# Two more blocks of an attention softmax moved from batched passes to head-by-head ScalarE exponentials

## The chip, the core and the metric

The kernel runs on one core of a Trainium2 chip. The metric is the device time of one execution in microseconds (us). TensorE is called PE here, its weight loads PEld, VectorE DVE, ScalarE ACT, GpSimd POOL, and SyncE, which issues most of the DMAs, SP.

## The reference

What is computed, cut to its three stages: attention over pooled keys and values, a gated feed-forward layer, and eight experts mixed by a normalised table.

```python
# 1 attention: batch 4, 8 heads, 576 queries, keys and values averaged in groups of 8 (72 left)
scores = scale * q @ k_p.T
scores = scores - max(scores, axis=-1)
attn = exp(scores); attn = attn / (sum(attn, axis=-1) + 1e-9)
x = attn @ v_p                                   # 2304 tokens x 512
# 2 gated layer: 512 -> 1536 -> 512
x = (sigmoid(x @ w_gate) * (x @ w_val)) @ w_out
# 3 eight experts of width 1024, weights P from 8 rounds of row and column normalisation
out = sum over e of P[:, e] * (relu(x @ w1[e]) @ w2[e])
```

Only the softmax of the first stage is touched by the change.

## The kernel before

Tokens are handled in six blocks of 384 (`NBLK`, `TB`), each of three tiles of 128 tokens (t = 0, 1, 2). Each tile has eight heads in two groups of four (g = 0, 1). So one block has six score groups. A score group fills 128 x 4 x 72 numbers of one PSUM bank.

All products of the gated layer are done in split precision: an operand is rounded to a high part (by ACT) and the rest is a low part (a subtraction by DVE or POOL), and `mm` does three matmuls for each pair. For a weight chunk of 128x512 the rounding is L231 (`wa_hi`) and the subtraction L236 (`wa_lo`), both in `split_chunk`. The 36 chunks of the gated layer's weights arrive as 64-bit numbers and must first be narrowed to 32 bits. That is done by `narrow_tick` in several ticks per chunk: DVE L165 to L175, an add L179 (POOL for the first 12 chunks, DVE for the others) and a scaling by ACT, L185. When a chunk has been rounded, it is also stored to DRAM (`narrow`, issued from ACT's queue) so that later blocks can read it back (`stage`).

The gated layer runs in 72 steps (j, f), block j against slice f of the hidden width. Their order begins with (0,0), (0,1), (0,2), (0,3), (1,2), (1,3), (1,0), (1,1), (2,0), (2,1); I call these steps 0 to 9. A step is: 12 matmuls for the gate ("g", L268), a sigmoid on ACT (L817), 12 for the value ("v", L268), their product on DVE (L820), its rounding on ACT (L821) and the low part on DVE (L824); then the 12 matmuls of the step before into the output (`x2_step`, L560).

The attention of block 0 runs ahead of all steps. The attention of the other blocks is a Python generator, `attention`, whose stages are slipped between the parts of the steps by `slot`, which is called three times in a step: after the sigmoid, after the value part, and after `x2_step`. In each slot first the narrowing ticks are placed, as long as an estimate of DVE's due time (`until`) is not too far ahead of PE's. Then stages are placed by credit: each slot adds (23 less the stages done) / (3 x steps left to the block's nominal first step, less the slot's number, less 3), and each stage costs one credit. `hold` can forbid stages before a given step. At the start of a step whose block isn't ready, all remaining stages of that block are placed at once. Engines work strictly in the order in which the program was written out, so this placing sets every queue's order.

The stages of a block j > 0 before the change: (for a new batch) two stages of key pooling (L320) and two of value pooling (L329); six stages `scores`, in which each stage first runs the `less_max` of the group before; then the stages of the softmax; then for each tile `divide`, two transposes (`turn_a`, L422, with a copy by ACT, L424), and `values` (L437), whose result ACT and DVE split into `xs`, which the matmuls of the block's steps read.

In `less_max`, block 0 takes the negated maximum of the group on DVE and then runs four exponentials on ACT, one for each head, straight from PSUM with the maximum as bias; each gives the row's sum as a by-product. Blocks 1 to 5 take the maximum (L369) and subtract it (L370) on DVE into the tile `e`; one exponential over the block's whole `e` (L393) is put in the list `later`, and three sums on DVE (`total`, L397), `invert` and `divide` (L407) follow.

PSUM banks for the attention while steps run come from the tag "at", which has two, used in turn; a bank comes free when its group has been read. `e` has one buffer, `den` two, and the narrowed chunk `made` four, each released by its store to DRAM.

Of the kernel before, what the change touches and what calls it, by code (L numbers as in the profile page):

```python
# [20 lines left out]
def attention_moe_moe_kernel(  # L21
# [112 lines left out]
    later = []  # L134
# [154 lines left out]
    now = [0]  # L289
    hold = [0]  # L290

    def attention(at):
        kp, vp, qs, krs, vrs = {}, {}, {}, {}, {}
        e_ts, dens, a_ts = {}, {}, {}

        def load_k(b, hp):
            krs[b, hp] = at.tile([128, SP, POOL], F32, tag="kr", name="kr", bufs=4)
            nc.sync.dma_start(
                out=krs[b, hp].rearrange("p s j -> p (s j)"), in_=k[b, :, hp * S : (hp + 1) * S]
            )  # L300

        def load_v(b, i):
            vrs[b, i] = at.tile([SP, 2 * D, POOL], F32, tag="vr", name="vr", bufs=4)
            nc.sync.dma_start(
                out=vrs[b, i].rearrange("p d j -> p (d j)"), in_=v[b, :, 2 * i * DM : 2 * (i + 1) * DM]
            )
# [8 lines left out]
        def pool_k(b, hp):  # L315

            if hp == 0:
                kp[b] = at.tile([128, HP, SP], F32, tag="kp", name="kp", bufs=2)
            until["dve"] += 750
            nc.vector.tensor_reduce(out=kp[b][:, hp], in_=krs.pop((b, hp)), axis=AX.X, op=ALU.add)  # L320
            if hp == HP - 1:
                nc.scalar.activation(out=kp[b], in_=kp[b], func=AF.Copy, scale=SCALE)

        def pool_v(b, i):

            if i == 0:
                vp[b] = at.tile([SP, DM], F32, tag="vp", name="vp", bufs=2)
            until["dve"] += 1150
            nc.vector.tensor_reduce(  # L329
                out=vp[b][:, 2 * D * i : 2 * D * (i + 1)], in_=vrs.pop((b, i)), axis=AX.X, op=ALU.add  # L330
            )
# [7 lines left out]
        def scores(j, t, g):  # L339


            if (t, g) == (0, 0):
                e_ts[j] = at.tile([128, TPB, H, SP], F32, tag="e", name="e", bufs=1)
                dens[j] = at.tile([128, TPB, H], F32, tag="den", name="den", bufs=2)
            e_t = e_ts[j][:, t, 4 * g : 4 * g + 4]
            pt = at_bank()
            sc = pt[:, 0 : 4 * SP].rearrange("p (h s) -> p h s", h=4)
            for c0, c1, b in pieces(j, t):
                for i in range(4):
                    pr = slice(64 * g, 64 * g + 64)  # L350
                    nc.tensor.matmul(  # L351
                        out=sc[c0:c1, i],
                        lhsT=qs[j, t][pr, i, c0:c1],
                        rhs=kp[b][pr, i],
                        start=True,
                        stop=True,
                    )
            if g:
                del qs[j, t]
            elif (j, t) != (0, 0):  # L360
                load_q(j + (t + 3) // TPB, (t + 3) % TPB)
            m = at.tile([128, 4], F32, tag="mx", name="mx", bufs=4)
            until["pe"] += 900
            until["dve"] += 950
            post.append(lambda: less_max(j, t, g, sc, m, e_t))

        def less_max(j, t, g, sc, m, e_t):
            if j:
                nc.vector.tensor_reduce(out=m, in_=sc, axis=AX.X, op=ALU.max)  # L369
                nc.vector.tensor_sub(out=e_t, in0=sc, in1=m.unsqueeze(2).to_broadcast([128, 4, SP]))  # L370
                return
            nc.vector.tensor_reduce(out=m, in_=sc, axis=AX.X, op=ALU.max, negate=True)
            for i in range(4):
                nc.scalar.activation(
                    out=e_t[:, i],
                    in_=sc[:, i],
                    func=AF.Exp,
                    bias=m[:, i : i + 1],
                    accum_out=dens[j][:, t, 4 * g + i : 4 * g + i + 1],
                )  # L380
# [4 lines left out]
        def flush():  # L385
            while post:
                post.pop(0)()
# [3 lines left out]
        def softmax(j):  # L391
            e_t = e_ts[j]
            nc.scalar.activation(out=e_t, in_=e_t, func=AF.Exp)  # L393

        def total(j, t):
            until["dve"] += 700
            nc.vector.tensor_reduce(out=dens[j][:, t], in_=e_ts[j][:, t], axis=AX.X, op=ALU.add)  # L397

        def invert(j, t):
            until["dve"] += 500  # L400
            den = dens[j][:, t]
            nc.vector.tensor_scalar_add(out=den, in0=den, scalar1=EPS)
            nc.vector.reciprocal(out=den, in_=den)

        def divide(j, t):
            until["dve"] += 750
            nc.vector.tensor_tensor(  # L407
                out=e_ts[j][:, t],
                in0=e_ts[j][:, t],
                in1=dens[j][:, t].unsqueeze(2).to_broadcast([128, H, SP]),  # L410
                op=ALU.mult,
            )

        def turn_a(j, t, g):

            if g == 0:
                a_ts[j, t] = at.tile([SP, H, 128], F32, tag="a", name="a", bufs=3)
            pt = at_bank()
            pa = pt[:SP].rearrange("p (h s) -> p h s", h=4)
            until["pe"] += 500  # L420
            for i in range(4):
                nc.tensor.transpose(out=pa[:, i], in_=e_ts[j][:, t, 4 * g + i], identity=ident)  # L422
            a_t = a_ts[j, t][:, 4 * g : 4 * g + 4]
            post.append(lambda: nc.scalar.copy(out=a_t, in_=pa))  # L424
# [71 lines left out]
        for j in range(1, NBLK):  # L496
            b = (j * TB + TB - 1) // S
            if (j * TB - 1) // S < b:
                for hp in range(0, HP, 2):
                    pool_k(b, hp)  # L500
                    pool_k(b, hp + 1)
                    yield None
                for i in range(4):
                    pool_v(b, i)
                    if i % 2:
                        yield None
            for t in range(TPB):
                for g in range(2):
                    scores(j, t, g)
                    yield None  # L510
                    flush()
            later.append(lambda j=j: softmax(j))
            hold[0] = now[0] + 1 + (j > 1)
            yield None
            while later:
                later.pop(0)()
            total(j, 0)
            total(j, 1)
            yield None
            total(j, 2)  # L520
            invert(j, slice(0, TPB))
            divide(j, 0)
            yield None
            divide(j, 1)
            yield None
            divide(j, 2)
            nb = ((j + 1) * TB + TB - 1) // S
            if j + 1 < NBLK and nb > b:
                for hp in range(HP):
                    load_k(nb, hp)  # L530
                for i in range(4):
                    load_v(nb, i)
            for t in range(TPB):
                for g in range(2):
                    turn_a(j, t, g)
                    yield None
                    flush()
                yield j
                values(j, t)
                if t < TPB - 1:  # L540
                    yield None
                flush()
            yield -1
# [183 lines left out]
    with tc.manual_schedule():  # L727
# [4 lines left out]
        at = at_pool.__enter__()  # L732
        pools["at"] = at
        stages = attention(at)
        mark = [None]
        n_ready = [0]
# [379 lines left out]
```

## Time and profile before

| | us |
|---|---|
| Median of 3 runs | 2191.98 |
| Lowest and highest run | 2191.56, 2198.58 |
| The profiled execution, its own time | 2192.21 |
| Span of its trace | 2190.4 |
| PE busy | 2091.4 |
| DVE busy | 1422.9 |
| ACT busy | 882.3 |
| POOL busy | 890.9 |

The profile is one execution. A busy PE is not one at its peak, so the granted clock of each stretch is read beside it: 1.0 stands for 2.4 GHz, and lower mean values of a stretch contain time at 1.2 GHz. Where an engine was idle, the trace names the engine and line that ended the wait. The 1.8 us between span and time lie outside of the trace.

### The profile page before, as it was taken

The page shows a single profiled execution, that of the slowest core. Times are in us where ns is not written, and L with a number is a line of the kernel's source. Part 1 is how long each engine was busy: PE and PEld are TensorE (multiplying, and loading weights), DVE is VectorE, ACT ScalarE, POOL GpSimd, SP SyncE. Part 2 cuts the span into 40 slices and gives each one's busy share as a digit, 9 for nine tenths or more (in the row PEclk, how much of TensorE's full clock was granted, in tenths as well). Part 3 has the DMA queues.
Part 4 walks back from the last instruction along what each step waited for, and adds up shares of the span by engine and source line. Part 5 has one row for each costly group of instructions (what it writes and reads, how often), then busy time and mean ns, then how long its engine had stood idle before and what let it go on. Part 6 is the DMA issues. An engine that isn't in the chain of part 4 may idle for free.

```text
span 2190.4 us, 28664 instructions
## 1 busy us (share of the span) xinstructions
PE 2091.4 (95%) x10973; PEld 1899.3 (87%) x10973; DVE 1422.9 (65%) x2172; ACT 882.3 (40%) x1607; POOL 890.9 (41%) x780
## 2 busy tenths in 40 slices
PE   4579998999999999999999999999999999999999
PEld 4468988988997888888888888989898989898988
DVE  6746876645434877666666666666666666666665
ACT  4234333454544344434343434343434343434342
POOL 1100000254554465454545454545454545454441
PEclk8689999999999999999999999999999999999999
DMA  7432553453572232121215121212125212121211
GB/s 228 151 112 81 164 168 106 130 172 117 191 242 75 75 116 77 58 78 58 78 58 207 58 77 58 78 58 78 58 77 180 85 58 78 58 78 58 77 58 39
DMA packets 87450, 222.09 MB, mean 101 GB/s; under 512 B 8848, under 2 KB 8848, under 8 KB 87312
## 3 DMA queue, kind: packets, MB, share of 16 engines
q1 hardware_dynamic: 82128, 210.81, 28.7%
q10 hardware_dynamic: 5184, 9.44, 1.2%
q8 instruction: 86, 1.41, 0.3%
q14 instruction: 52, 0.43, 0.1%
HBM read 189.55 MB, written 30.67 MB: 101 GB/s over the span
## 4 chain that ended last, share of the span: by engine, by line
PE 87%; DVE 7%; issue 2%; ACT 2%; DMA 1%; POOL 0%; SPq 0%; ACTq 0%; DVEq 0%; POOLq 0%
PE big L932 36%; PE at L901 18%; PE gv L901 14%; PE gv L268 11%; PE big L560 5%; DVE wa_lo L236 1%; PE at L351 1%; PE at L437 1%; DVE made L166 1%; DVE wide L175 1%; PE at L422 1%; DVE g L820 1%; DMA narrow<-made 0%; DVE den L397 0%; ACT wa_hi L231 0%
## 5 line engine op out<-in xcount | busy, mean ns | idle before, releaser
L932 PE MATMUL big<-w2hl,h 128*128 128x512 f32 x3456 | 893.7, 394 | 0.0
L932 PEld LDWEIGHTS big<-w2hl,h 128*128 128x128 f32 x3456 | 641.9, 188 | 102.6
L961 DVE SCALAR_TENSOR_TENSOR acc<-big,prob,acc 128x512 f32<-128x512 f32 x516 | 385.6, 747 | 265.2 <-PE big L932 259.1
L705 POOL TENSOR_TENSOR fa<-raw,fa 128x768 fp32r<-128x768 f32 x96 | 179.5, 1869 | 442.1 <-PE big L932 403.3
L268 PE MATMUL gv<-xs,wa_hi 128*128 128x384 f32 x1152 | 310.6, 351 | 19.5 <-ACT xs L447 8.0
L707 POOL TENSOR_TENSOR fs<-ss,fs 128x512 fp32r<-128x512 f32 x96 | 125.0, 1302 | 292.5 <-ACT fs L704 292.5
L915 ACT ACTIVATE h<-gv 128x384 fp32r<-128x384 f32 x192 | 94.3, 491 | 356.9 <-DVE gv L1043 196.2
L268 PEld LDWEIGHTS gv<-xs,wa_hi 128*128 128x128 f32 x1152 | 214.4, 196 | 26.2 <-ACT xs L447 8.8
L901 PE MATMUL at<-xf,fa 128*128 128x384 f32 x1152 | 233.4, 337 | 0.8 <-DVE c L1036 0.8
L901 PE MATMUL at<-xf,fs 128*128 128x384 f32 x1152 | 232.3, 336 | 0.4 <-ACT c L1009 0.4
L901 PE MATMUL gv<-xf,fs 128*128 128x384 f32 x1152 | 232.3, 337 | 0.0
L717 DVE TENSOR_TENSOR w2hl<-raw,w2hl 128x512 fp32r<-128x512 f32 x192 | 227.5, 1186 | 6.3 <-ACT w2hl L716 6.3
L901 PEld LDWEIGHTS at<-xf,fa 128*128 128x128 f32 x1152 | 206.4, 188 | 17.7 <-DVE c L1036 1.6
L268 PE MATMUL gv<-xs,wa_lo 128*128 128x384 f32 x576 | 200.8, 349 | 20.6 <-DVE wa_lo L236 18.6
L901 PEld LDWEIGHTS gv<-xf,fs 128*128 128x128 f32 x1152 | 206.1, 189 | 16.4 <-issue 0.2
L901 PEld LDWEIGHTS at<-xf,fs 128*128 128x128 f32 x1152 | 204.4, 188 | 9.0 <-ACT c L1009 0.7
L916 DVE SCALAR_TENSOR_TENSOR h<-gv,h 128x384 fp32r<-128x384 f32 x192 | 107.1, 558 | 107.7 <-ACT h L915 107.7
L560 PE MATMUL big<-h,wa_hi 128*128 128x384 f32 x576 | 150.8, 343 | 0.0
L594 POOL TENSOR_TENSOR fx<-x,fx 128x768 fp32r<-128x768 f32 x10 | 18.4, 1844 | 318.6 <-DVE x L577 266.8
L268 PEld LDWEIGHTS gv<-xs,wa_lo 128*128 128x128 f32 x576 | 112.9, 196 | 25.0 <-DVE wa_lo L236 22.6
L236 POOL TENSOR_TENSOR wa_lo<-stage,wa_hi 128x512 fp32r<-128x512 f32 x67 | 99.1, 1494 | 82.4 <-ACT wa_hi L231 69.0
L821 ACT ACTIVATE h<-g 128x384 fp32r<-128x384 f32 x72 | 37.8, 525 | 222.9 <-DVE g L820 222.9
(149 smaller groups left out, 2766.4 us busy)
## 6 DMA issues: line engine op xcount, KB each, us to landing
raw<-in_moe_w_dram SPq DMA_DIRECT2D x192, 512.0 KB, 4.1
stage<-narrow SPq DMA_DIRECT2D x150, 256.0 KB, 3.0
xd<-fx SPq DMA_DIRECT2D x21, 768.0 KB, 3.7
xf<-xd SPq DMA_DIRECT2D x21, 768.0 KB, 6.3
narrow<-made ACTq DMA_DIRECT2D x36, 256.0 KB, 2.6
wide<-in_moe_w_gate_dram SPq DMA_DIRECT2D x12, 512.0 KB, 3.7
wide<-in_moe_w_val_dram SPq DMA_DIRECT2D x12, 512.0 KB, 5.1
wide<-in_moe_w_out_dram SPq DMA_DIRECT2D x12, 512.0 KB, 7.4
```

What stands on the lines that cost most here:

```text
L236: eng.tensor_tensor(out=lo, in0=raw, in1=f32(hi), op=ALU.subtract)
L268: nc.tensor.matmul(out=out_, lhsT=a[s], rhs=b[m], start=(i == 0), stop=(i == n - 1))
L560: nc.tensor.matmul(out=x2p[d][:, :TB], lhsT=w[s][:, d * 128 : (d + 1) * 128], rhs=gs[j, f][m], start=(first and i == 0), stop=(last and i ...
L705: pl(out=fa[:, 1], in0=raw[:, 0:3], in1=f32(fa[:, 0]), op=ALU.subtract)
L707: pl(out=fs[:, 1, 0:2], in0=ss[:, 0:2], in1=f32(fs[:, 0, 0:2]), op=ALU.subtract)
L717: nc.vector.tensor_sub(out=t[:, 1, i], in0=raw[:, i], in1=f32(t[:, 0, i]))
L821: nc.scalar.activation(out=hi, in_=g, func=AF.Copy)
L901: nc.tensor.matmul(out=pt[:, :TB], lhsT=w[:, s, i, k], rhs=t[:, o, k], start=(start and m == 0), stop=(m == 5), skip_group_check=True,)
L915: nc.scalar.activation(out=t[:, 0], in_=src, func=AF.Relu)
L916: nc.vector.scalar_tensor_tensor(out=t[:, 1], in0=src, scalar=0.0, in1=f32(t[:, 0]), op0=ALU.max, op1=ALU.subtract)
L932: nc.tensor.matmul(out=py, lhsT=h[:, s, cs], rhs=w2hl[n][:, o, fh], start=(m == 0), stop=(m == 5))
L961: nc.vector.scalar_tensor_tensor(out=acc[t], in0=py, scalar=pr, in1=acc[t], op0=ALU.mult, op1=ALU.add)
```

## The change

Blocks 1 and 2 take the way of block 0: `less_max` now compares j with a constant `WHOLE` = 3. For these two blocks the subtraction on DVE is gone; four exponentials on ACT read the score bank, with the maximum as bias, and give the sums. The block-wide exponential, the three sums, their place in `later` and the `hold` are gone for them, and so is one of the two stages that held them; the other is left as an empty `yield`. Blocks 3 to 5 are as before.

```diff
     def attention(at):
+        WHOLE = 3
 ...
         def less_max(j, t, g, sc, m, e_t):
-            if j:
+            if j >= WHOLE:
                 nc.vector.tensor_reduce(out=m, in_=sc, axis=AX.X, op=ALU.max)
                 nc.vector.tensor_sub(out=e_t, in0=sc, in1=m.unsqueeze(2).to_broadcast([128, 4, SP]))
                 return
 ...
-            later.append(lambda j=j: softmax(j))
-            hold[0] = now[0] + 1 + (j > 1)
-            yield None
-            while later:
-                later.pop(0)()
-            total(j, 0)
-            total(j, 1)
-            yield None
-            total(j, 2)
+            if j >= WHOLE:
+                later.append(lambda j=j: softmax(j))
+                hold[0] = now[0] + 1 + (j > 1)
+                yield None
+                while later:
+                    later.pop(0)()
+                total(j, 0)
+                total(j, 1)
+                yield None
+                total(j, 2)
+            else:
+                yield None
             invert(j, slice(0, TPB))
             divide(j, 0)
             yield None
```

## Rows read from the trace of the kernel before

**Rows 1.** The page: engine totals, then PE and its granted clock in 40 slices

```profile
PE 2091.4 (95%) x10973; PEld 1899.3 (87%) x10973; DVE 1422.9 (65%) x2172; ACT 882.3 (40%) x1607; POOL 890.9 (41%) x780
...
PE   4579998999999999999999999999999999999999
...
PEclk8689999999999999999999999999999999999999
```

**Rows 2.** Waits of PE, 60 to 250 us: total us, times, longest us

```profile
PE at L422 <- DVE e L407: 19.1, 2, 11.6
PE gv L268 <- DVE wa_lo L236: 9.1, 5, 5.0
```

**Rows 3.** PE in order of time: start, us, what, [idle before, releaser]

```profile
92.86 0.44 PE L268 MATMUL gv<-xs,wa_lo 128*128 128x384 f32 x1 [2.48 <-DVE wa_lo L236]
...
106.46 1.04 PE L422 MATMUL at<-ident,e 128*72 128x128 f32 x4 [11.57 <-DVE e L407]
...
159.16 1.04 PE L422 MATMUL at<-ident,e 128*72 128x128 f32 x4 [7.50 <-DVE e L407]
```

**Rows 4.** ACT and its queue in order of time, 94 to 127 us

```profile
94.98 0.49 ACT L817 ACTIVATE g<-gv 128x384 f32<-128x384 f32 x1 [5.27 <-PE gv L268]
95.12 0.33 ACTq L233 DMA_DIRECT2D narrow<-made  x1
...
98.92 1.28 ACT L393 ACT_TABLE_LOAD   x1
100.22 1.64 ACT L393 ACTIVATE e<-e 128x1728 f32<-128x1728 f32 x1
...
126.20 1.28 ACT L817 ACT_TABLE_LOAD   x1 [3.05 <-PE gv L268]
```

**Rows 5.** DVE in order of time, 99 to 108 us

```profile
99.44 0.43 DVE L165 TENSOR_SCALAR made<-wide 128x512 uint32<-128x512 uint32 x1 [2.07 <-DMA narrow<-made]
...
102.91 2.06 DVE L397 TENSOR_REDUCE den<-e 128x8 f32<-128x576 f32 x3
...
105.56 2.10 DVE L407 TENSOR_TENSOR e<-e,den 128x576 f32<-128x576 f32 x3
```

**Rows 6.** Tile `e` by form: times, duration ns min/median/max, first and last start

```profile
L370 DVE TENSOR_TENSOR e<-at,mx x30: 457/458/459, 61.2 to 521.8; 128x288 f32<-128x288 f32 x30
...
L393 ACT ACTIVATE e<-e x5: 1643/1649/1650, 100.2 to 528.8; 128x1728 f32<-128x1728 f32 x5
```

**Rows 7.** ACT in block 0: first exponentials of the first and second group

```profile
10.97 0.32 ACT L374 ACTIVATE e<-big,mx 128x72 f32<-128x72 f32 x1 [2.56 <-DVE mx L372]
...
12.17 0.33 ACT L374 ACTIVATE e<-gv,mx 128x72 f32<-128x72 f32 x1
```

**Rows 8.** ACT in order of time, steps 1 and 2

```profile
57.03 0.66 ACT L185 ACTIVATE wide<-wide 128x512 f32<-128x512 f32 x1
57.58 0.62 ACT L231 ACTIVATE wa_hi<-made 128x512 fp32r<-128x512 f32 x1
...
81.52 0.49 ACT L817 ACTIVATE g<-gv 128x384 f32<-128x384 f32 x1 [10.41 <-PE gv L268]
```

**Rows 9.** DVE in order of time, steps 1 and 2

```profile
60.70 0.44 DVE L369 TENSOR_REDUCE mx<-at 128x4 f32<-128x288 f32 x1
...
63.67 0.68 DVE L236 TENSOR_TENSOR wa_lo<-made,wa_hi 128x512 fp32r<-128x512 f32 x1
...
83.20 0.69 DVE L236 TENSOR_TENSOR wa_lo<-made,wa_hi 128x512 fp32r<-128x512 f32 x1 [2.00 <-ACT wa_hi L231]
...
89.14 0.45 DVE L369 TENSOR_REDUCE mx<-at 128x4 f32<-128x288 f32 x1
```

**Rows 10.** PE in order of time: the first matmuls of step 8

```profile
181.80 0.51 PE L268 MATMUL gv<-xs,wa_hi 128*128 128x384 f32 x2
```

**Rows 11.** DVE, then PE in order of time, around 210 us

```profile
210.26 2.33 DVE L329 TENSOR_REDUCE vp<-vr 72x128 f32<-72x1024 f32 x2
...
213.12 0.61 PE L268 MATMUL gv<-xs,wa_hi 128*128 128x384 f32 x2 [2.50 <-DVE g L820]
```

**Rows 12.** Busy us of each engine from 210 to 220 us, granted clock, DMA

```profile
210.00:220.00 10.00, 7.50 (x36) 7.36 (x36) 6.41 (x11) 2.84 (x6) 0.00 (x0) 0.83 0.20 54
```

## The prediction

> **What bounds the kernel now.** I read the page's totals and slices first. PE is busy for 2091.4 of 2190.4 us, and all slices that are not full lie among the first ones, where the granted clock is lower too [rows 1]. So after the first 200 us or so the kernel is a full PE, and a change in the early attention can only move the start of that. Next I read who made PE wait there: from 60 to 250 us the two longest items are the transposes waiting for `divide`, 19.1 us in two waits, and gate or value matmuls waiting for the low part of a weight chunk, 9.1 us in five [rows 2]. The two waits are the softmaxes of blocks 1 and 2: 11.57 us ahead of 106.46 and 7.50 us ahead of 159.16 [rows 3]. These are the waits that the change works on.
>
> What fills the 11.57 us decides what they are worth. In it ACT loads a table (1.28), does the block's exponential (1.64) [rows 4]; but DVE is not waiting for that. It waits 2.07 us for a store of a narrowed chunk, then does one tick with its low part, from 99.44 to 102.91 (3.47 us), and only then the three sums (2.06), the inversion, and the first of three divides [rows 5]. So most of this wait is narrowing that has to be done anyway; about 3 us are softmax.
>
> **The change part by part.** *DVE.* Gone are 12 subtractions; in a row of them one takes 0.46 us [rows 6], some 0.1 of which overlaps its neighbours, so 12 x 0.37 = 4.4 us. Gone are six sums, 2 x 2.06 = 4.1 us [rows 5]. In all 8.5 us from an engine that is the early bottleneck.
>
> *ACT.* Gone are two exponentials of 1.65 us [rows 6]. Added are 48 of one head each. Block 0 does just this operation: the first group starts at 10.97 and the second at 12.17, so a group of four costs 1.20 us with the reads of its sums [rows 7]; 12 groups are 14.4 us. ACT has the room on average; what counts is who stands behind them in its queue.
>
> *Order.* The planner's credits can be worked out from the code. In step 2 they are, slot by slot, 14/9, 13/8 and 12/7 on top of what was left: 1.93, 2.55 and 3.27. Before, the second slot placed the stage with the last maximum and `hold` kept the rest (3.27) back until the first slot of step 3, where four stages came at once, up to the first transpose: this is why it stands behind step 3's gate. Now the 2.55 buy two stages. Done for all slots, this gives the new order. The six score groups of block 1 keep their places: one after the gate part of step 1, three in step 2's run-up, one in step 2's first slot, one in its second. The sigmoid of step 2 therefore falls between the fourth and fifth group, that of step 3 behind the sixth. Without `hold` the inversion and first divide follow the sixth group at once, two divides and the first transpose come in the third slot of step 2, ahead of step 3's gate matmuls and not behind them. In block 2 the sigmoids enclose all six groups; its divides come in the first slot of step 5, not of step 6, and its last `values` at the end of step 6, not in step 7. Block 3's pooling then starts with 2.96 credits in step 7 where it had 1.28, which puts its stages some six slots (two steps) earlier.
>
> *Tables.* Sigmoid and exponential need different tables: a switch is 1.30 us from load to next start (98.92 to 100.22) [rows 4]. Block 2 keeps two switches. Block 1 had two (at 98.92 and 126.20) and gets four: exponential ahead of groups 1 and 5, sigmoid in steps 2 and 3. The load of a sigmoid is exposed: at 126.20 it started only when PE's gate matmuls were done [rows 4]. Whether the load of an exponential also follows the wait for the maximum isn't shown by any row. If it comes first it is hidden, because ACT stands idle there; if not it costs 1.30. I take 0.4 for each, nearer to hidden, since the exponentials of block 0 wait in the instruction itself for one engine [rows 7]; both ends go into the range.
>
> The Trainium skill (ScalarE: Activation LUTs, What ACT_TABLE_LOAD costs) puts a switch at about 2.66 us, because it counts a drain of 1.38 us beside the load of 1.28, and its rule is to batch calls by table set. That rule speaks against this change, which alternates the sets twice as often in block 1. The trace has the load's 1.28 and no drain of its own. By the page's figure the four switches of block 1 would cost 1.36 us more each if all were exposed, and the sum below would come to about 2192.4.
>
> *Block 1, walked through.* (a) Group 1's exponentials stand ahead of L185 and L231 for step 1's value part. The maximum ends at 61.15 [rows 9]; 1.20 for the group, 0.55 to L231 and 0.62 for it [rows 8] give 63.5, where DVE is ready at 63.67 [rows 9]: nothing, or 1.2 with an exposed load. (b) Groups 2 to 4 hand banks on by exponentials in place of subtractions and stand ahead of the next L231: 0.5 to 1.7 later at step 2's gate. (c) The sigmoid of step 2 (81.52) [rows 8] gets its load, 1.3; L236 of its value part waits for ACT already (2.00 at 83.20) [rows 9], so this is all on the path: 1.8 to 2.9. (d) Group 5 stands ahead of the rounding of g times v, so the last maximum, at 89.14 [rows 9], comes at 91.1 to 93.5. Then 1.2 for the group, about 0.5 inversion, 0.7 divide [rows 5]: the first transpose starts at 94.2 to 96.6 in place of 106.46. (e) That looks like 10 us, but two divides (1.4), a tick and its low part now stand ahead of step 3's gate: it starts its low parts at 98.3 to 100.8, not 92.86 [rows 3], 5.4 to 7.9 late. (f) Its sigmoid gets a load of 1.3. The store that DVE waits for was issued at 95.12, right behind that sigmoid, and held DVE until 99.44, 4.3 later [rows 4, 5]. So the next tick starts at 104.7 to 109.7 and ends 3.5 later. Step 3's product then is 2.6 us earlier to 3 us later than before. (g) What is left of the block (transposes and values with ACT's copies between) is bound to step 4 as before. Block 1 in sum: 1 us earlier to 3.3 us later, taken +1.2.
>
> *Block 2.* No narrowing stands in its wait, so the softmax chain counts: load 1.28 and exponential 1.65 [rows 4, 6] and sums 2.06 [rows 5] go, 5.0 us; the last group's 1.20 [rows 7] comes in. That is 3.8 of the 7.50 us [rows 3]. The groups' banks are handed on later (some 1 us), and the earlier start leaves no transposes for step 7 (some 1 us back). I take -4.0, with ends 0 and -6.
>
> *After step 8.* Step 8 starts at 181.80 [rows 10] and PE is full from there, so the sum of the two shifts everything behind. One thing more moves: block 3's value pooling. At 210.26 two such reductions (2.33 us) stand ahead of step 11's product, and PE then waits 2.50 us [rows 11] and runs at a mean clock of 0.83 in these 10 us, 1.7 us of work lost [rows 12]. Two steps earlier DVE has room. In their place come a maximum and a subtraction (0.9). I take -2.5, with ends 0 and -4.2.
>
> Sum: +1.2 - 4.0 - 2.5 = -5.3. On the profiled execution's 2192.2 us, which stands 0.2 above the median, this gives 2186.9, so 2187.
>
> **The rivals.** *Bounded elsewhere, no change (2190 to 2194, taken 2192.5).* The weight narrowing between 195 and 345 us could be held by its stores and loads and not by the steps; then an early gain is waited away there. For it: the store wait of 2.07 [rows 5]. Against it: from 200 us on PE waits mainly for DVE's results [rows 11]. The same time comes out when every switch empties ACT first and costs twice its 1.30: two exposed loads of sigmoids and two of exponentials make +5.2, and 2187 becomes 2192. The skill's figure for a switch, named above, is this case; the trace doesn't bear it out.
>
> *Slower: ACT's queue and PE's clock (2199).* The place is step 3 and step 5, where the transpose now stands ahead of matmuls that used to run first. All loads are exposed (block 1 at +3.3), and PE, which stands idle before and after that transpose, runs at 1.2 GHz. A run of 12 matmuls is 2.0 us at full clock (92.86 to the sigmoid at 94.98) [rows 3, 4] and so twice that at half; gate, value and output part of step 3 and value, output and gate of steps 5 and 6 would be six of these, +12, of which two (behind 106.46 and 159.16) pay before as well: +8. With block 2 at -3 and nothing behind: +3.3 + 8 - 3 = +8.3, or 2200; with half of the later gain 2199. It decides when these idle times leave the lower clock for more than one part. For it: the slices of 8, 6 and 8 in the clock [rows 1]. Against it: the wait of 2.48 us at 92.86 didn't lower the clock, and step 3's gate took 2.0 us.
>
> *It does what the DVE sum says (2181).* If all 8.5 us of DVE's work come out, loads are hidden and the later stall goes: -8.5 - 2.5 = -11.
>
> That it doesn't do what it says is excluded as far as I can see: block 0 has the same code.
>
> **How the numbers follow.** The forecast (2183 to 2190) has 0.5, no change 0.2, slower 0.18, the larger gain 0.12. A difference under 0.3%, 6.6 us, can't be told from none here. Below 2185.4 lie a good four tenths of the forecast and the larger gain, 0.34; above 2198.6 lies most of the slower case, 0.14; the rest, 0.52, is within. Leaving out a tenth at each end gives 2180 to 2200. The likeliest case's own range is 2183 to 2190.
>
> **What would show it right or wrong.** Right: no wait of over 6 us ahead of the transposes; ACT loads at groups 1 and 5 and at the sigmoids of steps 2 and 3; the first transpose of block 1 before 97; step 3's gate late by 5 to 8 us; step 4 starting within 1 earlier and 3.3 later of before, step 8 at 176 to 182; no 2.5 us wait at step 11. An exponential's load that starts before its maximum is done settles the first unknown. Wrong: a granted clock of a half through all of steps 3 and 5; new waits at 300 to 345 us that take the gain back; score matmuls waiting for banks by more than 2 us a group.

## The result, and the profile after

The changed kernel takes 2213.47 us (median of 4 runs, 2210.99 to 2213.83) against 2193.27 of the kernel before on the same chip: a ratio of 1.0083, 95% interval 1.0067 to 1.0099. It is slower by 0.8%, some 18 us by the ratio. The forecast was 2187 with a range up to 2200; the time lies outside of it, on the side of the rival "slower".

The page of the changed kernel: engine totals, PE in 40 slices, its granted clock.

```profile
PE 2110.2 (95%) x10973; PEld 1916.1 (87%) x10973; DVE 1412.4 (64%) x2154; ACT 896.5 (41%) x1703; POOL 889.7 (40%) x780
...
PE   4678998999999999999999999999999999999999
...
PEclk8678999999999999999999999999999999999999
```

DVE did lose its work (1422.9 to 1412.4; 10.5 us less, predicted 8.5) and ACT gained 14.2 beside [rows 1] (the prediction's terms make 13.7: 14.4 for the groups and 2.6 for two more table loads, less 3.3 for the two block-wide exponentials). But PE, with the same 10973 matmuls, is busy for 18.8 us longer, and its fourth slice (166 to 221 us) has a lower share than before. The granted clock goes with this: its mean over the execution is 0.970, before it was 0.980.

Next, who made PE wait between 60 and 250 us, in the changed kernel (total us, times, longest us).

```profile
PE gv L268 <- ACT wa_hi L231: 11.9, 4, 7.3
PE at L438 <- ACT a L425: 8.6, 6, 3.0
PE at L352 <- ACT e L375: 8.5, 4, 3.4
PE gv L268 <- DVE wa_lo L236: 3.0, 2, 2.3
PE gv L268 <- DVE g L824: 2.4, 1, 2.4
PE at L423 <- DVE e L408: 2.3, 1, 2.3
```

Of the kernel before, in the same stretch, beside [rows 2]:

```profile
PE at L437 <- ACT a L424: 3.3, 5, 1.2
PE at L351 <- DVE e L370: 3.0, 2, 2.2
...
PE gv L268 <- ACT wa_hi L231: 0.7, 1, 0.7
```

The 19.1 us of transposes waiting for `divide` [rows 2] are 2.3. In their place stand three waits for ACT: the rounding of weights (L231, 11.9 for 0.7), the copies (L425, 8.6 for 3.3), and the exponentials that hold the score banks (L375, 8.5, where subtractions by DVE held them for 3.0). DVE's waits became ACT's waits.

Where the 18 us sit is seen from the start of each step's sigmoid in ACT's order of time. The table gives by how much a kernel's step comes later than in the kernel before, as differences over stretches of steps (us, one profiled execution each; the last column is the comparison of all runs).

| kernel | start to step 0 | 0 to 4 | 4 to 8 | 8 to 30 | 30 to 71 | ratio to before |
|---|---|---|---|---|---|---|
| after | +1.0 | +1.6 | +10.0 | +7.4 | +4.8 | 1.0083 |
| e1 carry cut | -0.1 | +4.9 | -1.7 | -17.1 | +2.3 | 0.9923 |
| e2 block 1 alone | +0.8 | +5.0 | +1.9 | +3.0 | 0.0 | 1.0019 |
| e3 block 2 alone | +0.4 | +4.9 | +1.4 | -18.2 | +2.3 | 0.9927 |
| e4 old places | +0.3 | +6.0 | -2.2 | +0.4 | 0.0 | 1.0020 |
| e7 carry cut, block 3 late | +0.2 | +4.7 | -4.0 | +1.6 | +7.8 | 1.0018 |
| e5 before, block 3 early | +0.8 | +0.5 | +0.2 | -17.9 | +3.5 | 0.9917 |
| e6 after, block 3 early | +1.2 | +3.9 | +13.6 | -17.8 | +3.2 | 0.9971 |
| e9 before, tanh | -1.4 | -0.3 | -1.2 | +2.2 | -3.5 | 0.9959 |
| e10 after, tanh | -1.0 | +2.3 | +3.0 | +4.7 | +0.9 | 1.0021 |
| e11 as e7, tanh | -1.2 | +2.5 | -1.9 | +2.0 | +0.9 | 0.9991 |

The column "0 to 4" scatters: an experiment that leaves block 1 untouched (e3, below) has +4.9 there with the same operations as before; 3.1 of it come between the sigmoids of steps 3 and 4, where PE ran at half clock (0.50 from 122 to 130 us, 1.00 in the kernel before). It bears no weight. The next two columns scatter by 1 to 5 us: e8, the same kernel as e10, has +4.0 and -0.3 there. A row needn't add up to its ratio: the kernel before took 2192.2 us in its profiled execution, under the medians that the ratios go by (2193.3 to 2195.8), the profiled executions of e2, e3, e6 and e7 are the slowest of theirs (e6's is 6.0 above its median), and the changed kernel gets 3.1 us back behind step 71. The changed kernel's loss stands in three places: steps 4 to 8, a stall of 7.4 us at steps 16 to 18, and 4.7 us between steps 48 and 54.

PE of the changed kernel in order of time, steps 2 to 5 (start, us, what, idle before and its releaser).

```profile
98.41 1.04 PE L423 MATMUL at<-ident,e 128*72 128x128 f32 x4 [2.27 <-DVE e L408]
...
102.38 0.69 PE L268 MATMUL gv<-xs,wa_lo 128*128 128x384 f32 x1 [2.29 <-DVE wa_lo L236]
...
128.75 0.51 PE L268 MATMUL gv<-xs,wa_hi 128*128 128x384 f32 x2
...
129.27 0.51 PE L268 MATMUL gv<-xs,wa_hi 128*128 128x384 f32 x2
...
129.88 1.62 PE L352 MATMUL at<-kp,qt 64*128 64x72 f32 x16
134.90 1.98 PE L352 MATMUL at<-kp,qt 64*128 64x72 f32 x8 [3.40 <-ACT e L375]
137.93 0.84 PE L268 MATMUL gv<-xs,wa_hi 128*128 128x384 f32 x2
...
138.89 0.84 PE L268 MATMUL gv<-xs,wa_hi 128*128 128x384 f32 x2
...
140.94 1.98 PE L352 MATMUL at<-kp,qt 64*128 64x72 f32 x8
145.17 1.98 PE L352 MATMUL at<-kp,qt 64*128 64x72 f32 x8 [2.25 <-ACT e L375]
```

ACT over the same steps: the loads of the change, and the first two groups of block 2.

```profile
62.11 1.28 ACT L375 ACT_TABLE_LOAD   x1 [4.09 <-DVE mx L373]
...
85.91 1.28 ACT L821 ACT_TABLE_LOAD   x1 [5.45 <-PE gv L268]
...
89.85 1.28 ACT L375 ACT_TABLE_LOAD   x1
92.81 0.32 ACT L375 ACTIVATE e<-at,mx 128x72 f32<-128x72 f32 x1 [1.67 <-DVE mx L373]
...
105.76 1.28 ACT L821 ACT_TABLE_LOAD   x1 [7.78 <-PE gv L268]
...
132.23 1.28 ACT L375 ACT_TABLE_LOAD   x1 [1.17 <-DVE mx L373]
133.53 0.32 ACT L375 ACTIVATE e<-at,mx 128x72 f32<-128x72 f32 x1
...
157.06 1.28 ACT L821 ACT_TABLE_LOAD   x1 [2.01 <-PE gv L268]
```

DVE: the product of step 4.

```profile
141.05 0.56 DVE L824 TENSOR_TENSOR g<-g,gv 128x384 f32<-128x384 f32 x1 [8.53 <-PE gv L268]
```

Read together: in step 4 two score groups of block 2 follow the gate (129.88), and a third (134.90) stands ahead of the value matmuls. That one needs a bank that the first group holds until ACT has loaded its table (132.23) and done four exponentials (133.53 on). PE idles 3.40 us, and then the same matmuls come at little over half the pace: three of them follow each other in 0.96 us (137.93 to 138.89), where the gate of the same step took 0.52 (128.75 to 129.27). The value part ends so late that DVE idles 8.53 us.

What the 10.0 us of steps 4 to 8 are is seen from the two kernels between these steps' sigmoids (busy times of PE, PEld, DVE, ACT and POOL, the granted clock, DMA share and GB/s), first the kernel before,

```profile
127.49:184.13 56.64, 43.43 (x252) 39.73 (x252) 25.78 (x46) 21.33 (x36) 0.00 (x0) 0.85 0.40 120
...
132.00:142.00 10.00, 9.15 (x38) 8.44 (x39) 3.56 (x8) 2.31 (x5) 0.00 (x0) 0.52 0.39 128
```

then the changed one.

```profile
130.05:196.69 66.64, 54.15 (x266) 49.45 (x267) 19.75 (x35) 26.81 (x82) 0.00 (x0) 0.72 0.31 94
...
134.00:156.00 22.00, 18.85 (x65) 17.39 (x66) 4.26 (x10) 10.06 (x52) 0.00 (x0) 0.50 0.50 153
```

PE idles no longer than before (12.5 us for 13.2); all of the 10 us is busy time at a lower clock. PE at half clock is nothing new in step 4: the kernel before has it from 132 to 142 us (0.52). But there it lasts 10 us, and in the changed kernel 22. What was a wait for DVE is paid for in PE's clock.

### The profile page after: what moved, and what is told of

Its sections match the earlier page's. It is cut to its first block, busy times and chain, and to the rows that moved or that the text cites. A ratio compares the mean times of both kernels' runs of the same rounds, so it can differ in the third digit from the quotient of the medians.

```text
span 2212.0 us, 28743 instructions
## 1 busy us (share of the span) xinstructions
PE 2110.2 (95%) x10973; PEld 1916.1 (87%) x10973; DVE 1412.4 (64%) x2154; ACT 896.5 (41%) x1703; POOL 889.7 (40%) x780
## 4 chain that ended last, share of the span: by engine, by line
PE 88%; DVE 5%; ACT 3%; issue 2%; DMA 1%; POOL 0%; SPq 0%; ACTq 0%; DVEq 0%; POOLq 0%
PE big L936 36%; PE at L905 18%; PE gv L905 14%; PE gv L268 12%; PE big L564 5%; PE at L352 1%; DVE wa_lo L236 1%; PE at L438 1%; ACT wa_hi L231 1%; DVE made L166 1%; PE at L423 0%; DVE g L824 0%; DVE wide L175 0%; ACT e L375 0%; PE at L268 0%
## 5 line engine op out<-in xcount | busy, mean ns | idle before, releaser
L268 PE MATMUL gv<-xs,wa_hi 128*128 128x384 f32 x1152 | 320.9, 361 | 30.2 <-ACT wa_hi L231 18.3
L268 PEld LDWEIGHTS gv<-xs,wa_hi 128*128 128x128 f32 x1152 | 222.8, 204 | 37.8 <-ACT wa_hi L231 21.2
L711 POOL TENSOR_TENSOR fs<-ss,fs 128x512 fp32r<-128x512 f32 x96 | 125.0, 1302 | 293.1 <-ACT fs L708 293.1
L268 PE MATMUL gv<-xs,wa_lo 128*128 128x384 f32 x576 | 206.4, 358 | 16.6 <-DVE wa_lo L236 14.7
L268 PEld LDWEIGHTS gv<-xs,wa_lo 128*128 128x128 f32 x576 | 116.9, 203 | 21.2 <-DVE wa_lo L236 18.8
L712 POOL TENSOR_TENSOR fs<-ss,fs 128x512 fp32r<-128x512 f32 x96 | 125.4, 1307 | 0.0
```

What stands on the lines that cost most here:

```text
L268: nc.tensor.matmul(out=out_, lhsT=a[s], rhs=b[m], start=(i == 0), stop=(i == n - 1))
L711: pl(out=fs[:, 1, 0:2], in0=ss[:, 0:2], in1=f32(fs[:, 0, 0:2]), op=ALU.subtract)
L712: pl(out=fs[:, 1, 2:4], in0=ss[:, 2:4], in1=f32(fs[:, 0, 2:4]), op=ALU.subtract)
```

## The experiments

My theory after the trace: the planner's credit, not the exponentials, puts the third score group ahead of step 4's value part and block 3 one slot later, and both cost. The rival: the exponentials and their table loads on ACT cost what is lost, wherever the stages stand.

**e1: the credit carried into step 4 cut to the old value.** Nothing else of the changed kernel is touched.

```diff
                 n_stage[0] = 0
+                credit[0] = min(credit[0], 0.35)
```

> The changed kernel with one number altered: when block 1 is forced ready at step 4, the planner's leftover credit is cut to 0.35, its value in the kernel before. The first slot of step 4 then places two score groups of block 2 and not three, so the third stands behind step 4's value matmuls again. Theory O (the order is the cause: the third group waits for a bank that four exponentials and a table load hold, PE idles 3.4 us and falls to half clock, and all of steps 4 and 5 is behind it): the loss of 10 us between steps 4 and 8 shrinks to 0 to 4, the time to 2200 to 2206. Rival X (the exponentials and table loads on ACT cost this wherever they stand): 2209 to 2214.

Measured: 2178.71 us, ratio 0.9923 (0.9906 to 0.9939), over 20 us under what either theory expected. One number in the planner is worth 34.8 us (2213.47 less 2178.71), and the changed operations, so ordered, are faster than the kernel before. Score groups in step 4 of e1 (PE in order of time):

```profile
137.12 1.11 PE L352 MATMUL at<-kp,qt 64*128 64x72 f32 x8 [1.09 <-ACT e L375]
140.49 3.19 PE L352 MATMUL at<-kp,qt 64*128 64x72 f32 x16 [2.27 <-ACT e L375]
```

The third group now stands behind the value part and waits 1.09 us in place of 3.40. But most of the gain isn't there: of the difference to the changed kernel 11.7 us lie in steps 4 to 8 and 24.5 in steps 8 to 30. In e1 block 2 ends with 2.87 credits left, so block 3's stages come some six slots earlier. So e1 mixes two things, and e5 to e7 take them apart.

**e2 and e3: one block alone.** e2 changes block 1 only (`WHOLE = 2`), e3 block 2 only (the condition `j not in (0, 2)` in both places).

> Only block 1 on the new way (WHOLE = 2); blocks 2 to 5 as before. The changed kernel starts step 4 only 2.6 us later than before, 0.9 of it from the loading of the first keys. Theory O: block 1 costs 0 to 3 us and leftover credit 0.7 now brings the third group of block 2 ahead of step 4's value matmuls, but there its bank is handed on by a subtraction, which costs little: 2192 to 2197. Rival X: half of the loss is block 1's: 2200 to 2204.

> Only block 2 on the new way; block 1 as before, so that the leftover credit at step 4 is the old one and the third group stands behind the value matmuls. Theory O: block 2's operations cost -4 to +3 here: 2188 to 2196. Rival X: they bring their 10 us and what follows later: 2202 to 2212.

Measured: e2 2199.96, ratio 1.0019 (1.0007 to 1.0031); e3 2179.79, ratio 0.9927 (0.9910 to 0.9944). Neither theory had e3; e2 lies just under the rival's range and 3 us over the theory's. Block 1 alone costs 4 us; block 2 alone gains 16. Block 2 can't have such a gain by its own stages: it is in steps 8 to 30 again (-18.2), where e3's block 3 starts early. The two don't add up to the change. The carried credit is block 1's and is there in e2 as well: e2's third group of block 2 also stands ahead of step 4's value matmuls. But in e2 its bank is handed on by a subtraction; PE of e2 idles 1.24 us ahead of it, where the profile names no engine that it waited for,

```profile
135.95 1.89 PE L352 MATMUL at<-kp,qt 64*128 64x72 f32 x8 [1.24 <-issue]
```

and its steps 4 to 8 lose 1.9 us and not 10. In e3 the exponentials are there and the place isn't. Only the change has both.

**e4: the new operations in the old places.** `later`, `hold` and both extra stages stay; only what they hold is left out for blocks 1 and 2.

```diff
-            if j >= WHOLE:
-                later.append(lambda j=j: softmax(j))
-                hold[0] = now[0] + 1 + (j > 1)
-                yield None
+            if j >= WHOLE:
+                later.append(lambda j=j: softmax(j))
+            hold[0] = now[0] + 1 + (j > 1)
+            yield None
 ...
```

> New operations in the old places: blocks 1 and 2 take the exponentials head by head, but the two stages and the hold stay, empty of sums and of the block-wide exponential, so that divides, transposes and all later blocks keep the slots of the kernel before. Theory O: what is left is the gain of the missing sums and subtractions less exposed table loads and later banks: 2186 to 2195. Rival X: 2202 to 2212, since all ACT work of the change is there.

Measured: 2200.59, ratio 1.0020 (1.0009 to 1.0031), between the two expectations. Places kept, the exponentials on ACT bring nothing and cost about 4 us.

**e5: the kernel before with block 3's early start alone.** No operation is changed; in `slot`, where block 2's last stage is done, its credit is set.

```diff
                     n_stage[0] = n_stage[0] + 1 if n_ready[0] == j else 0
+                    if n_ready[0] == 3 and j == 2:
+                        credit[0] = 3.0
```

> The kernel before with one number altered: when block 2 is done (first slot of step 7) the planner's credit is set to 3, so that block 3's pooling and scores start some six slots earlier, as in the two kernels that came out at 2179 us; no operation is changed. Theory P (the 17 us that those two gain between steps 8 and 30 come from the early start of block 3 alone): 12 to 18 us under the kernel before, 2177 to 2184. Rival E (they need the DVE work that the change removes): within 5 us of the kernel before.

Measured: 2178.29, ratio 0.9917 (0.9890 to 0.9943). The whole gain of e1 is had without a single changed exponential. Where it comes from: PE's waits from 186 to 372 us, of the kernel before,

```profile
PE gv L268 <- DVE wa_lo L236: 7.8, 5, 2.9
PE gv L268 <- ACT wa_hi L231: 3.6, 3, 1.7
PE gv L268 <- DVE g L820: 3.4, 3, 2.5
```

and of e5,

```profile
PE gv L268 <- DVE g L822: 2.2, 1, 2.2
PE gv L268 <- DVE wa_lo L236: 0.8, 1, 0.8
```

and busy times of PE, PEld, DVE, ACT and POOL in two stretches, the granted clock, DMA share and GB/s, of the kernel before,

```profile
186.00:230.00 44.00, 41.20 (x230) 40.16 (x229) 34.21 (x58) 17.19 (x35) 0.00 (x0) 0.96 0.30 100
...
310.00:360.00 50.00, 42.39 (x236) 40.35 (x237) 29.97 (x54) 14.79 (x29) 0.00 (x0) 0.93 0.32 108
```

and of e5.

```profile
186.00:230.00 44.00, 44.00 (x259) 42.70 (x259) 39.12 (x70) 18.46 (x38) 0.00 (x0) 1.00 0.40 128
...
310.00:360.00 50.00, 48.49 (x299) 46.03 (x299) 36.03 (x61) 20.57 (x39) 3.69 (x2) 1.00 0.37 130
```

In the kernel before PE is not full behind step 8. It waits 14.8 us in these eleven waits, all for operands that DVE or ACT makes late, and its clock falls below 1.0 around them. With block 3's value pooling at 184.70 and 189.16 us and not at 200.21 and 210.26, DVE is busier (39.12 for 34.21 of 44 us), PE is full, and the waits for such operands shrink to 3.0 us. By the starts of the sigmoids 4.7 us of it are gained in steps 9 to 18 and 12.4 in two jumps, at steps 26 (-7.4) and 29 (-5.0), where the kernel before waited for the last narrowed weights from 308 to 345 us. That the earlier pooling brings these weights forward is seen from DVE's last narrowing tick, in the kernel before (step 28's sigmoid starts at 332.9) and in e5 (322.2).

```profile
338.41 0.42 DVE L165 TENSOR_SCALAR made<-wide 128x512 uint32<-128x512 uint32 x1
...
321.81 0.42 DVE L165 TENSOR_SCALAR made<-wide 128x512 uint32<-128x512 uint32 x1
```

It stands 5.5 us behind step 28's sigmoid before and 0.4 ahead of it in e5. As `narrow_tick` is placed by the planner's estimate of DVE's due time, the pooling's place moves the ticks in the program too; how much is this and how much DVE's freed time isn't tested.

**e6: the changed kernel, order of step 4 kept, block 3 early.** In the same place the credit is set to 2.6 and `hold` to step 7.

> The changed kernel, unaltered up to the end of block 2 (third score group ahead of step 4's value matmuls), and then block 3 held to step 7 with a credit of 2.6, so that it starts six slots earlier than in the changed kernel. Theory P: the loss of 10 us between steps 4 and 8 stays, and behind step 8 some 17 us are gained where the changed kernel lost 9: 2187 to 2196. Rival E: within 5 us of the changed kernel's 2213.

Measured: 2188.66, ratio 0.9971 (0.9956 to 0.9986). In its profile steps 4 to 8 still lose (+13.6) and steps 8 to 30 change by -17.8. From step 7 on, e6 has the slots of e1; the two differ in the place of step 4's third group and what shifts with it up to step 6. By all runs that is 10 us (2188.66 less 2178.71), the cleanest measure of the order of step 4, with the table loads in it. The loss in step 4 and the place of block 3 are separate.

**e7: carry cut as in e1, and block 3 in its old slots** (credit 0.7 where e5 sets 3.0).

> As the run with the leftover credit cut at step 4, and in addition the credit is cut to 0.7 when block 2 is done, so that block 3 starts in the slots of the kernel before. Theory P: the step 4 to 8 part stays at -2 to 0, the 17 us behind step 8 are gone: 2192 to 2199. Rival E: 2177 to 2182 as without the second cut.

Measured: 2199.84, ratio 1.0018 (1.0006 to 1.0029), 1 us over the theory's range. Steps 4 to 8 gain 4.0, steps 8 to 30 nothing (+1.6). In its profile 6.5 of the 7.8 us behind step 30 come between steps 48 and 54: block 5's softmax has also moved by a slot, from the end of step 50 to the start of step 51. `hold` then keeps it to step 53 and not 52, four stages come at once, and PE waits 3.79 us for its divide at 548.38, where the kernel before waits 0.7. That is a second effect of the credit that I set, not of the exponentials.

**e8 to e11: no table switch.** With tanh in place of sigmoid (another activation is computed) no load is left but the one at the start; the order is not touched. e8 is a single run of the changed kernel so altered; e9 is the same edit on the kernel before, e10 the kernel of e8 with more runs, e11 the edit on e7.

```diff
-                    nc.scalar.activation(out=g, in_=pg[:, :TB], func=AF.Sigmoid)
+                    nc.scalar.activation(out=g, in_=pg[:, :TB], func=AF.Tanh)
```

> The changed kernel with the sigmoid of the gated layer replaced by tanh, which changes what is computed there and only that; if it lies in the exponential's table set, no ACT table load is left behind the first. Theory O: the third group's wait at step 4 is 3.4 us with the load of 1.28 in it, so without loads it is near 2.1, and with the two sigmoid loads of block 1 gone the time falls by 3 to 8 us, to 2205 to 2210. Rival T (the alternation of table sets is what costs the 20 us): 2190 to 2198.

> The kernel before, with the tanh in place of the sigmoid of the gated layer (so the activation computed is another one); order and all other operations as in the kernel before. It is the base for the next two. In the kernel before the loads stand at four places in blocks 1 and 2, hidden or in waits for the transposes (1.28 each). If loads in themselves cost PE nothing unless they lengthen a wait, this is 0 to 3 us under the kernel before: 2191 to 2195, with the sigmoid of step 4 up to 1.3 us earlier. If each load were on the path it would be some 5 us under it.

> The changed kernel, with tanh in place of sigmoid (as the one look before, now with rounds): no table loads within the steps, the order with the third score group of block 2 ahead of step 4's value matmuls kept. Loads lengthening PE's waits to where the clock falls: 2193 to 2198, and steps 4 to 8 some 4 us longer than in the kernel before, not 10. If the one look was chance and order is the cause by itself: 2205 to 2212.

> The changed kernel with the carried credit cut at step 4 (so the third score group of block 2 stands behind step 4's value matmuls) and block 3's stages in their old slots, with tanh in place of sigmoid: neither the loads nor the order. With loads, this order took 2199.8. If the exposed loads make its 4.5 us, 2192 to 2196, within 2 us of the base with tanh. If order and loads each cost by themselves, it lies under the changed kernel with tanh by over 5 us: under 2190. If the loads alone decide in steps 4 to 8, it lies within 3 us of the changed kernel with tanh.

Measured: e8 2194.65 (one run); e9 2186.82, ratio 0.9959 (0.9945 to 0.9974); e10 2199.03, ratio 1.0021 (1.0011 to 1.0030); e11 2193.26, ratio 0.9991 (0.9980 to 1.0001). e8's one time lies just under the ten of e10, which is the same kernel (2194.89 to 2201.81). In us (ratio differences by 2195; each is good to some 3 us):

| | with loads | without | the loads |
|---|---|---|---|
| before | 0 | -9 | 9 |
| operations changed, carry cut, block 3 in its old slots (e7, e11) | +4 | -2 | 6 |
| as changed (after, e10) | +18 | +5 | 14 |
| the order's part (last less second) | 14 | 7 | |

Neither theory stands alone. The order (step 4's and block 3's slot together) costs 7 us without any load and 14 with them: the third group then also waits for the load. In steps 4 to 8 alone all runs fall into place (us against the kernel before, one profiled execution each):

| block 2's groups | third group behind step 4's value matmuls | ahead of them |
|---|---|---|
| subtractions | 0 (before) | +1.9 (e2) |
| exponentials, table loads | -4.0 (e7), -2.2 (e4), -1.7 (e1), +1.4 (e3) | +10.0 (after), +13.6 (e6) |
| exponentials, no loads | -1.9 (e11) | +3.0 (e10), +4.0 (e8) |

In these steps the place alone costs little and the operations alone nothing. With the exponentials the place costs some 5 us without loads and 9 to 18 with them. PE's wait ahead of the third group in e10:

```profile
132.38 1.98 PE L352 MATMUL at<-kp,qt 64*128 64x72 f32 x8 [2.12 <-ACT e L375]
```

2.12 for 3.40: the load's 1.28 are just the difference. The same holds for the other two executions with this order (1.03 us in e8 and 2.31 in e6). From 144 to 160 us the granted clock is 0.82 in e10 and 0.61 in the changed kernel, though PE waits twice there in e10 (1.12 and 1.24 us) and once in the changed kernel (2.25). My expectation for e9 missed: I took the loads of the kernel before for hidden (0 to 3 us), and they are worth 9 in all, 1.4 of them ahead of step 0 and the others spread over all blocks. e8 is in the range that was expected if the loads are the cause, e10 between the two ranges, 1 us over that of the loads. e11 missed as well: it is in the range for exposed loads (2192 to 2196) but 6 us over e9 and not within 2.

**The other two places.** PE of the changed kernel at steps 17 and 18, and in block 5's softmax:

```profile
263.19 0.69 PE L268 MATMUL gv<-xs,wa_lo 128*128 128x384 f32 x1 [2.35 <-DVE wa_lo L236]
...
268.46 1.01 PE L268 MATMUL gv<-xs,wa_hi 128*128 128x384 f32 x2 [1.70 <-ACT wa_hi L231]
...
562.68 1.04 PE L423 MATMUL at<-ident,e 128*72 128x128 f32 x4 [3.86 <-DVE e L408]
```

Block 2 ends with 0.12 credits in the changed kernel, so block 3 starts a slot later than before. DVE then does narrowing and block 3's maxima in steps 16 and 17 together, and the weights come late. The stall is there with loads and without (step 16 to 18: +7.4 in after and in e10, +4.3 in e8), and smaller where the slots are the old ones (+0.7 in e7, +2.0 in e11, and +2.1 in e9), so it is the order's. Which of DVE's work in these steps is the late one I read from the trace and didn't test. Block 5's shift by a slot, as in e7, makes the wait at 562.68.

## Why the prediction was wrong, point by point

*The failed step: "Order", where it starts block 2 from no credit.* The replay of block 1 was right. But step 4 forces block 1's last stages, and the credit that is left is carried on to block 2: 0.72 after the change, 0.35 before. The prediction put this carry at nothing without a reason: its 2.96 credits in step 7, and block 2's divides in the first slot of step 5, come out of the code only from a credit of 0 at step 4. With the carry the first slot of step 4 has 23/9 and 0.72, so 3.28, three stages and not two. From this one fraction follow the third group ahead of step 4's value part, and a block 2 that ends with 0.12 credits, so that "block 3's pooling then starts with 2.96 credits in step 7" is false in its sign: it starts one slot later than before. e1 cuts the carry to 0.35 and has the order I wrote down to within a slot; it measures 34.8 us less than the change, 10 of it by step 4's order (e6 less e1) and most of the rest by block 3's place.

*"After step 8", -2.5 (0 to -4.2): the wrong sign for the change, and a term mis-sized by a factor of seven.* The early start that I predicted is worth -17 to -18 us where it does occur (e1, e3, e5, e6). I priced the one wait that I saw at step 11 [rows 11, 12] and took PE for full behind it. The page's slices there [rows 1] read 9, and one reads 8 (the seventh, 329 to 383 us), which "all slices that are not full lie among the first ones" passes over; each 9 hides up to a tenth, and eleven waits with the clock beside them lay in 186 to 372 us. So the first section's "after the first 200 us or so the kernel is a full PE" was wrong. Had the order been as written, the time would have been about that of e1, 2179, just under the range.

*Block 2, -4.0 (0 to -6): right in its own order, wrong in the real one.* e7 gives -4.0 and e1 -1.7 in steps 4 to 8 (e3 +1.4); the changed kernel +10.0. The banks "handed on later (some 1 us)" became PE waits of 3.40 and 2.25 and half clock behind them. I had named score matmuls that wait more than 2 us for banks as the sign of a wrong forecast; they are there, but it was no good sign: e1 and e3, two of the fastest kernels, have such waits too (2.27 us at 140.49 and 4.27 at 139.53).

*Block 1, +1.2 (-1 to +3.3): not refuted, and not resolved.* The changed kernel has +1.6 at step 4, inside, but e3 shows that this place scatters by 5 us. e2, block 1 alone, costs 4 us in all. By its steps, 0.9 us of each being there at step 1 already: (a) step 1's value part gets its low parts at 66.65, 2.2 later than the 64.41 before, so the exposed end; (c) step 2's sigmoid comes at 87.20, 5.7 after its place in [rows 8], where I had summed at most 2.9; (d) the first transpose at 98.41 in place of 106.46 [rows 3], not 94 to 97 (the terms written there make 93.5 to 95.9, 0.7 less than the 94.2 to 96.6 stated); (e) step 3's low parts at 102.38 in place of 92.86, 9.5 late where I had 5.4 to 7.9; (f) its product at 113.43, 2.1 later, inside my range.

*Tables.* I took exponentials' loads for nearly hidden (0.4 each). Of three, two started only behind the wait for the maximum (62.11, 132.23); at 89.85 it ran ahead and was hidden. The sigmoids' loads are all exposed, as assumed. The size of a load was right (1.30 from load to start); its effect was not, since the load at 132.23 lengthens a PE idle, and behind it PE ran at half clock from 134 to 156 us; in e10, without the load, it did from 132 to 138 and from 142 to 148. The Trainium skill (ScalarE: Activation LUTs, What ACT_TABLE_LOAD costs) has 2.66 us for a switch, with a drain; the rows here show a load of 1.28 and the next start 1.30 after the load's (62.11 to 63.41), as before the change, and the measurement decides. The rule of the Trainium skill to batch calls by table set (the same page, Table sets: the hidden batching unit) speaks against this change, and e9 agrees: the twelve loads that tanh takes out of the kernel before are worth 9 us.

*DVE's 8.5 us* are gone, and worth nothing where places are kept: e4 is 4 us slower than before, and so is e7, where block 5's shift is in it.

*The rivals.* "ACT's queue and PE's clock" (2199, chance 0.18) was the right mechanism: ACT's queue holds PE, and PE runs at half clock after it. I put it at the transposes of steps 3 and 5; it came at the score groups of step 4 and through step 5. "Bounded elsewhere" fell with e5: the narrowing follows the place of the stages (its last tick at 321.81 for 338.41). The faster case by DVE's sum fell with e4.

*What stays open.* Why the load at 89.85 ran ahead of its wait and the others didn't. And whether the operations cost anything at all with the places kept: e2, e4 and e7 are all 4 us over the kernel before, but in e4's profile these lie ahead of step 4, where e3 scatters as far without a changed block 1, and in e7's they lie in the shift of block 5.

The best kernel is the one before with block 3's early start (e5, 2178.29); e1 (2178.71) and e3 (2179.79) can't be told from it.

## What to carry to other kernels

Where a planner's running credit sets the order, replay it through every carry-over, to the end of the program, before pricing any operation: here one fraction of a stage was worth 35 us, and the operations by themselves cost some 4. Read "PE full" from the waits and the clock of each stretch, not from slices in tenths. An operation that moves to another engine also moves the release of the buffer that it reads; price the engine that waits for this buffer at its lower clock.

## What the runs showed of the hardware

A table load can be held behind the wait of the instruction that it serves (62.11, 132.23, 157.06) or run ahead of it (89.85); in both cases it takes 1.28 us. Exponentials of 128x72 with their sum read out follow each other at 0.29 to 0.30 us (93.12, 93.41 and 93.71 in ACT's order of time), so a group takes 1.2 as in block 0 [rows 7]. The length of one idle doesn't tell whether PE's clock falls: in the kernel before, PE waited 2.89 us at 342.00, and from 334 to 346 us the mean clock is 1.00; in e5 it waited 2.22 us at 288.20, and from there to 292 it is 0.55.
